# Decay attention and a softplus FFN on one core: TensorE's queue in emission order from the third block on

## The chip, the core and the metric

The kernel runs on one core of one Trainium2 chip. A core has five engines that work side by side, each through a queue of its own in strict program order: TensorE (PE, matrix products; its weight loads are shown as PEld), VectorE (DVE), ScalarE (ACT), GpSimd (POOL) and SyncE (SP, which here issues the DMAs). They meet at semaphores only. Matmuls write to PSUM, a small memory of eight banks, from which VectorE and ScalarE read. The metric is device microseconds of the whole program. "Faster" and "slower" mean against the kernel before.

## What is computed

For four sequences of 768 tokens and eight heads of 64, a linear attention with a decaying state is computed, and its output goes through a feed-forward network (FFN) with a softplus in the middle:

```python
for t in range(S):
    state = gamma[None, :, None, None] * state + np.einsum('bhd,bhe->bhde', k[:, :, t], v[:, :, t])
    y[:, :, t] = scale * np.einsum('bhd,bhde->bhe', q[:, :, t], state)
x = np.ascontiguousarray(attn_out.transpose(0, 2, 1, 3)).reshape(B * S, H * D)   # 3072 x 512
h = x @ w_in                                              # 512 -> 2048
g = np.maximum(h, 0.0) + np.log1p(np.exp(-np.abs(h)))     # softplus
return (g @ w_out).astype(np.float32)                     # 2048 -> 512
```

## The kernel before

**Units of attention.** The tokens are cut into 24 chunks of 128, and a unit is one chunk with four of its heads, 48 units in all. A unit passes through parts. `load_unit` and `decay` fetch q, k and v and scale them (L136, L153, L179, L180). `operands` turns k and q over on VectorE (L199) and splits them into high and low halves in one of two `kq` buffers (ScalarE L203, L206, L207; VectorE L204, L208). `scores` makes two score products `sc` on TensorE (L227), reduces each on VectorE (L228), masks the result on GpSimd (L229) and splits it into `ah` (ScalarE L233) and `al` (GpSimd L234). `new_state` adds to the running state in PSUM (L249). `outputs` makes the attention output `yp` on TensorE (L298 to L302; it reads `kq`, the state, `ah` and `al`), and ScalarE (L304, `xh`) and then VectorE (L306, `xl`) read it out of PSUM. `stack_state` copies the state out of PSUM (ScalarE L269, VectorE L271). The first 12 units go through simpler forms of these parts.

**Blocks of FFN.** The tokens are also cut into nine blocks: two of 256, six of 384 and one of 256. For a block of 384 there are 16 steps. A step's `hidden` is twelve matmuls into a buffer `hp` (L334 to L336); the softplus goes over VectorE (L341), ScalarE (L342), VectorE (L346), ScalarE (L348, `gh`) and GpSimd (L350, `gl`); and `second`, nine matmuls into three accumulators (L365 to L367), follows two steps later. At a block's end the accumulators are copied out (L379) and stored by DMA (L381).

**Interleaving.** The attention of a block runs beside the FFN of the block before it. `stages` (one call per step) emits `hidden`, about half of the step's ticks of attention, `second` of two steps before, and the other ticks. A unit takes four ticks: `operands`, `outputs` of the unit before, `scores`, `new_state`. Whole parts are emitted, one behind another.

**What sets the order in the queues.** The program is recorded in emission order, but a scheduler then lays out the instructions of each engine by a timeline of its own, in which an instruction that it expects to be ready may go ahead of one that it expects to wait. So an engine's queue differs from the emission order, and groups of matmuls are found inside one another. On the chip each queue is then fixed.

**PSUM.** `hp` has two banks, the accumulators three, the state one. `sc` and `yp` share the last two, the pool `ps_a`: each new tile takes one of the two, and its first matmul waits until the bank's last reader is done. Which of the two it takes is settled with the order.

```python
sc = ps_a.tile([P, 2, 2, C], F32, name="sc", tag="a")
yp = ps_a.tile([D, 2, NJ, C], F32, name="yp", tag="a")
```

Of the kernel before, what the change touches and what calls it, by code (L numbers as in the profile page):

```python
# [27 lines left out]
LAG = 2  # L28
# [5 lines left out]
def decay_attention_then_softplus_ffn(ctx: ExitStack, tc: tile.TileContext, q, k, v, w_in, w_out, qtab, vtab, gtab, out):  # L34
# [283 lines left out]
    def tick(n):  # L318
        for at, part in PARTS.items():
            u, r = divmod(n - at, PERIOD)  # L320
            if r == 0 and 0 <= u < len(units):
                part(u)
# [4 lines left out]
    def hidden(s):  # L327
        i, fs = steps[s]
        xh, xl = (x[:, :, spans[i][0]] for x in xring)
        hp = hps[s] = ps_h.tile([P, len(fs), BLOCKS[i]], F32, name="hp", tag="hp")  # L330
        for k, f in enumerate(fs):
            wt = win[f].rearrange("p t (c f) -> p t c f", c=ND)
            for d in range(ND):
                nc.tensor.matmul(hp[:, k], lhsT=wt[:, 0, d, :], rhs=xh[:, d, :], start=d == 0, stop=False)  # L334
                nc.tensor.matmul(hp[:, k], lhsT=wt[:, 0, d, :], rhs=xl[:, d, :], start=False, stop=False)  # L335
                nc.tensor.matmul(hp[:, k], lhsT=wt[:, 1, d, :], rhs=xh[:, d, :], start=False, stop=d == ND - 1)  # L336


    def softplus_1(s):
        sp = sps[s] = ffn.tile(list(hps[s].shape), F32, name="sp", tag="sp")  # L340
        nc.vector.tensor_scalar(sp.bitcast(U32), hps[s].bitcast(U32), 0x80000000, None, op0=ALU.bitwise_or)  # L341
        nc.scalar.activation(sp, sp, AF.Softplus)  # L342

    def softplus_2(s):
        g = sps[s]
        nc.vector.scalar_tensor_tensor(g, hps.pop(s), 0.0, g, op0=ALU.max, op1=ALU.add)  # L346
        gh = ffn.tile(list(g.shape), F32R, name="gh", tag="gh")
        nc.scalar.copy(gh, g)  # L348
        gl = ffn.tile(list(g.shape), F32R, name="gl", tag="gl")
        nc.gpsimd.tensor_tensor(gl, sps.pop(s), gh.bitcast(F32), op=ALU.subtract)  # L350
        gs[s] = gh, gl

    def second(s):
        i, fs = steps[s]
        NT = BLOCKS[i] // P
        gh, gl = gs.pop(s)
        begins = s == 0 or steps[s - 1][0] != i
        ends = s + 1 == len(steps) or steps[s + 1][0] != i
        if begins:
            acc[i] = [ps_o.tile([P, DM], F32, name=f"acc{t}", tag=f"acc{t}") for t in range(NT)]  # L360
        for k, f in enumerate(fs):
            wt = wout[f]
            for t in range(NT):
                ts = slice(t * P, (t + 1) * P)
                nc.tensor.matmul(acc[i][t], lhsT=gh[:, k, ts], rhs=wt[:, 0], start=begins and k == 0, stop=False)  # L365
                nc.tensor.matmul(acc[i][t], lhsT=gh[:, k, ts], rhs=wt[:, 1], start=False, stop=False)  # L366
                nc.tensor.matmul(acc[i][t], lhsT=gl[:, k, ts], rhs=wt[:, 0], start=False, stop=ends and f == fs[-1])  # L367
        if not ends:
            return
        for t in range(NT):  # L370
            if fs[-1] < NF - 1:
                part[i, t] = ffn.tile([P, DM], F32, name="part")
                (nc.scalar.copy if t % 2 else nc.vector.tensor_copy)(part[i, t], acc[i][t])
                continue
            o = ffn.tile([P, DM], F32, name="o", tag="o")
            if (i, t) in part:
                nc.vector.tensor_tensor(o, acc[i][t], part.pop((i, t)), op=ALU.add)
            else:
                (nc.scalar.copy if t % 2 else nc.vector.tensor_copy)(o, acc[i][t])  # L379
            row = int(FIRST[i]) + list(spans[i][1]).index(t) * P  # L380
            nc.sync.dma_start(out[row:row + P, :], o)  # L381
# [5 lines left out]
    steps = []  # L387
# [8 lines left out]
    done, loaded, converted = FIRST_TICK, 0, 0  # L396

    def convert_to(n):
        nonlocal loaded, converted
        while converted < min(NF, n):  # L400
            convert_weights(converted)
            converted += 1
            if loaded < NF:
                load_weights(loaded)
                loaded += 1
# [29 lines left out]
    def block_decays():  # L435
        own = (lo, slice(0, H, 2)), (up, slice(1, H, 2))
        for at in range(0, P, 32):
            for i in range(C // 32):
                nc.sync.dma_start(
                    qblocks[at:at + 32, 0, :, :, i].rearrange("p f m -> p (f m)"), qtab[i * 32:(i + 1) * 32, at // D:H:2]  # L440
                )
        for c in range(1, NC):
            for half, heads in own:
                old, new = (qblocks[half, t].rearrange("p f m i -> p (f m) i") for t in (c - 1, c))
                nc.gpsimd.tensor_tensor(new, old, gtab_sb[half, 0, heads].unsqueeze(2).broadcast_to(list(new.shape)), op=ALU.mult)
# [14 lines left out]
    plan = [0] * len(steps)  # L460
    for a, b in zip(starts, starts[1:]):
        i = steps[b][0]
# [8 lines left out]
    def stages(s, until):  # L471

        nonlocal done
        ok = lambda t: 0 <= t < len(steps)
        if ok(s):
            hidden(s)
            softplus_1(s)
            softplus_2(s)
        until = max(until, done)
        half = (done + until + 1) // 2  # L480
        while done < half:
            tick(done)
            done += 1
        if ok(s - LAG):
            second(s - LAG)
        while done < until:
            tick(done)
            done += 1

    for s, (i, fs) in enumerate(steps):  # L490
        if s == TURN:
            block_decays()
        convert_to(fs[-1] + 1)
        stages(s, plan[s])
        convert_to(2 * max(fs[-1] // 2 + 1, s + 1 if s < TURN else TURN + (s - TURN) // 2) + EARLY)
    for s in range(len(steps), len(steps) + LAG):
        stages(s, done)


# [28 lines left out]
```

## Time and profile before

| | |
|---|---|
| median of 3 runs | 683.71 us (682.54 to 686.89) |
| profiled execution | 683.14 us, of which the span is 681.3 us |
| TensorE busy | 661.6 us, 97% of the span |
| VectorE, ScalarE, GpSimd busy | 64%, 53%, 46% |
| granted TensorE clock | 0.997 on average |

A row of the timeline has start and length in us, engine, line, operation, what it writes and reads, how many were merged (xN), and in brackets the idle time ahead of it and what ended it. A matmul's length contains the time until its result has drained, so matmuls that follow one another overlap: the pace of TensorE is read from start to start. A row of the groups has, between the bars, the busy time in us and the mean in ns of one.

### The profile page before, as it was taken

The numbers are of one execution on the slowest core, as the hardware profiler recorded it, in microseconds if no ns is written. First come the engines' busy times: TensorE is split into PE (matmuls) and PEld (weight loads), VectorE is DVE, ScalarE is ACT, GpSimd is POOL, SyncE is SP. The second block draws the span as 40 slices with busy tenths as digits, with TensorE's granted clock in tenths as the row PEclk, the third lists the DMA queues.
The fourth block names the chain that finished last, engine by engine and source line by source line (L and its number), as shares of the span: only waits on it lengthen the run. The fifth ranks groups of instructions, "written<-read, shape, count | busy, mean of one in ns | idle before, by whom it ended". The sixth has DMA issues, their size and how long they took to land.

```text
span 681.3 us, 12857 instructions
## 1 busy us (share of the span) xinstructions
PE 661.6 (97%) x4146; PEld 600.3 (88%) x4146; DVE 436.1 (64%) x843; ACT 358.0 (53%) x808; POOL 316.5 (46%) x354
## 2 busy tenths in 40 slices
PE   7999899999999999999999999999999999999997
PEld 6898789988999999988999899988999899999996
DVE  5678698578567576785676766778666755432321
ACT  5788775545555355554555655455555545422221
POOL 5797666535435453454355344535344543332221
PEclk9999999999999999999999999999999999999999
DMA  9898653123112131222222222222212211000100
GB/s 246 237 270 231 184 141 72 26 69 82 35 36 53 29 95 26 40 39 64 48 38 54 37 77 42 37 36 53 76 37 38 36 33 47 1 1 1 46 1 32
DMA packets 153826, 46.75 MB, mean 69 GB/s; under 512 B 140448, under 2 KB 148640, under 8 KB 153760
## 3 DMA queue, kind: packets, MB, share of 16 engines
q1 hardware_dynamic: 153312, 45.93, 28.3%
q8 instruction: 33, 0.54, 0.3%
q14 instruction: 33, 0.27, 0.1%
q10 hardware_dynamic: 448, 0.01, 0.0%
HBM read 39.60 MB, written 6.29 MB: 67 GB/s over the span
## 4 chain that ended last, share of the span: by engine, by line
PE 52%; DVE 12%; SPq 11%; DMA 9%; issue 6%; ACT 5%; POOL 2%; DVEq 0%; ACTq 0%; POOLq 0%
SPq L136 10%; PE hp L334 8%; PE hp L336 8%; PE acc L365 8%; PE acc L367 8%; PE acc L366 8%; PE hp L335 8%; DVE kq L204 3%; DMA wout<-in_moe_w_out_dram 2%; DMA win<-in_moe_w_in_dram 2%; DMA kb<-in_k_dram 2%; DVE kq L208 2%; DMA qb<-in_q_dram 2%; DVE a L228 1%; DMA vn<-in_v_dram 1%
## 5 line engine op out<-in xcount | busy, mean ns | idle before, releaser
L350 POOL TENSOR_TENSOR gl<-sp,gh 128x384 fp32r<-128x384 f32 (+1 forms) x120 | 130.6, 1089 | 223.1 <-ACT gh L348 201.3
L334 PE MATMUL hp<-xh,winhl 128*128 128x384 f32 (+1 forms) x576 | 185.3, 322 | 2.4 <-DVE sp L346 1.9
L336 PE MATMUL hp<-xh,winhl 128*128 128x384 f32 (+1 forms) x576 | 184.7, 321 | 0.3 <-POOL winhl L99 0.3
L335 PE MATMUL hp<-xl,winhl 128*128 128x384 f32 (+1 forms) x576 | 183.7, 319 | 0.0
L365 PE MATMUL acc<-wouthl,gh 128*128 128x512 f32 x384 | 152.7, 398 | 0.0
L366 PE MATMUL acc<-wouthl,gh 128*128 128x512 f32 x384 | 151.8, 395 | 0.0
L367 PE MATMUL acc<-wouthl,gl 128*128 128x512 f32 x384 | 150.2, 395 | 0.0
L342 ACT ACTIVATE sp<-sp 128x384 f32<-128x384 f32 (+1 forms) x120 | 65.3, 546 | 137.7 <-DVE sp L341 134.6
L334 PEld LDWEIGHTS hp<-xh,winhl 128*128 128x128 f32 x576 | 108.8, 189 | 7.1 <-DVE sp L346 1.7
L335 PEld LDWEIGHTS hp<-xl,winhl 128*128 128x128 f32 x576 | 108.8, 189 | 3.7
L336 PEld LDWEIGHTS hp<-xh,winhl 128*128 128x128 f32 x576 | 108.7, 189 | 0.8 <-POOL winhl L99 0.5
L341 DVE TENSOR_SCALAR sp<-hp 128x384 uint32<-128x384 uint32 (+1 forms) x120 | 68.4, 573 | 61.1 <-PE hp L336 60.5
L348 ACT CAST gh<-sp 128x384 fp32r<-128x384 f32 (+1 forms) x120 | 64.1, 534 | 73.9 <-DVE sp L346 44.6
L346 DVE SCALAR_TENSOR_TENSOR sp<-hp,sp 128x384 f32<-128x384 f32 (+1 forms) x120 | 69.4, 580 | 34.6 <-ACT sp L342 33.6
L367 PEld LDWEIGHTS acc<-wouthl,gl 128*128 128x128 f32 x384 | 71.7, 188 | 14.4
L366 PEld LDWEIGHTS acc<-wouthl,gh 128*128 128x128 f32 x384 | 72.3, 188 | 11.1
L365 PEld LDWEIGHTS acc<-wouthl,gh 128*128 128x128 f32 x384 | 72.2, 188 | 10.9
L229 POOL TENSOR_SCALAR_AFFINE_SELECT a<-a 128x512 f32<-128x512 f32 x48 | 35.9, 749 | 48.5 <-DVE a L228 34.9
L228 DVE TENSOR_REDUCE a<-sc 128x256 f32<-128x512 f32 x72 | 48.9, 680 | 9.3 <-PE sc L227 7.8
L234 POOL TENSOR_TENSOR al<-a,ah 128x512 fp32r<-128x512 f32 x36 | 48.1, 1337 | 10.7 <-ACT ah L233 10.5
L204 DVE TENSOR_TENSOR kq<-kb,kq 64x256 fp32r<-64x256 f32 x72 | 49.7, 690 | 3.2 <-ACT kq L203 1.1
L199 DVE STREAM_TRANSPOSE kb<-kb 128x256 f32<-128x256 f32 x36 | 16.0, 445 | 51.8 <-DMA kb<-in_k_dram 39.8
(83 smaller groups left out, 994.0 us busy)
## 6 DMA issues: line engine op xcount, KB each, us to landing
win<-in_moe_w_in_dram SPq DMA_DIRECT2D x16, 512.0 KB, 4.5
wout<-in_moe_w_out_dram SPq DMA_DIRECT2D x16, 512.0 KB, 4.5
vn<-in_v_dram SPq DMA_DIRECT2D x48, 128.0 KB, 2.8
out_dram<-o SPq DMA_DIRECT2D x24, 256.0 KB, 2.1
kb<-in_k_dram SPq DMA_DIRECT2D x288, 16.0 KB, 1.7
qb<-in_q_dram SPq DMA_DIRECT2D x288, 16.0 KB, 1.7
vn<-in_k_dram SPq DMA_DIRECT2D x30, 128.0 KB, 2.4
qn<-in_q_dram SPq DMA_DIRECT2D x12, 128.0 KB, 4.7
```

Source lines behind the costliest of these rows:

```text
L136: nc.sync.dma_start(t[at:at + 32, h // 2], src[b, hf * HH + h, c * C:(c + 1) * C, d:d + 32].rearrange("(i t) d -> t i d", t=32))
L204: nc.vector.tensor_tensor(kq[oth, 0, par], kt[own], kq[own, 0, par].bitcast(F32), op=ALU.subtract)
L334: nc.tensor.matmul(hp[:, k], lhsT=wt[:, 0, d, :], rhs=xh[:, d, :], start=d == 0, stop=False)
L335: nc.tensor.matmul(hp[:, k], lhsT=wt[:, 0, d, :], rhs=xl[:, d, :], start=False, stop=False)
L336: nc.tensor.matmul(hp[:, k], lhsT=wt[:, 1, d, :], rhs=xh[:, d, :], start=False, stop=d == ND - 1)
L341: nc.vector.tensor_scalar(sp.bitcast(U32), hps[s].bitcast(U32), 0x80000000, None, op0=ALU.bitwise_or)
L342: nc.scalar.activation(sp, sp, AF.Softplus)
L346: nc.vector.scalar_tensor_tensor(g, hps.pop(s), 0.0, g, op0=ALU.max, op1=ALU.add)
L350: nc.gpsimd.tensor_tensor(gl, sps.pop(s), gh.bitcast(F32), op=ALU.subtract)
L365: nc.tensor.matmul(acc[i][t], lhsT=gh[:, k, ts], rhs=wt[:, 0], start=begins and k == 0, stop=False)
L366: nc.tensor.matmul(acc[i][t], lhsT=gh[:, k, ts], rhs=wt[:, 1], start=False, stop=False)
L367: nc.tensor.matmul(acc[i][t], lhsT=gl[:, k, ts], rhs=wt[:, 0], start=False, stop=ends and f == fs[-1])
```

## The change

The steps are split where the third block (index 2) begins. From there on the loop runs inside a manual schedule for TensorE: its instructions keep the order in which the kernel emits them. The other four engines are still ordered by the scheduler, against TensorE's new order. `convert_to` is not called in the second loop; all weights are converted by then. No instruction on tensors is added or removed, and the pools and buffers stay the same.

```diff
-    for s, (i, fs) in enumerate(steps):
+
+    ordered = next(s for s, (i, fs) in enumerate(steps) if i == 2)
+    for s, (i, fs) in enumerate(steps[:ordered]):
         if s == TURN:
             block_decays()
         convert_to(fs[-1] + 1)
         stages(s, plan[s])
         convert_to(2 * max(fs[-1] // 2 + 1, s + 1 if s < TURN else TURN + (s - TURN) // 2) + EARLY)
-    for s in range(len(steps), len(steps) + LAG):
-        stages(s, done)
+    with tc.manual_schedule(engines={mybir.EngineType.PE}):
+        for s in range(ordered, len(steps)):
+            stages(s, plan[s])
+        for s in range(len(steps), len(steps) + LAG):
+            stages(s, done)
```

How the queues move is shown at one unit, the eighteenth (`yp_2455` before, `yp_2457` now; a number behind a name tells one tile from another). TensorE before: the first matmul of `yp` stands inside a `second`, and the first score product of the next unit (`sc_2517`) inside the rest of it.

```order
L365 MATMUL acc2_2025<-wouthl_692,gh_2338 128x512
L300 MATMUL yp_2455<-ah_2374,vhl_2279 64x128
L366 MATMUL acc2_2025<-wouthl_692,gh_2338 128x512
L367 MATMUL acc2_2025<-wouthl_692,gl_2340 128x512
L227 MATMUL sc_2517<-kq0_84 128x256 x2
L334 MATMUL hp_2530<-xh_82,winhl_892 128x384
L335 MATMUL hp_2530<-xl_83,winhl_892 128x384
L336 MATMUL hp_2530<-xh_82,winhl_892 128x384
L301 MATMUL yp_2455<-al_2375,vhl_2279 64x128
```

The second product, `sc_2521`, stands behind the end of `yp_2455` and nine more matmuls of `hidden`; it waits for VectorE's reduction of `sc_2517`. TensorE now, from the last matmul of `yp` on:

```order
L302 MATMUL yp_2457<-ah_2376,vhl_2281 64x128
L365 MATMUL acc0_2025<-wouthl_692,gh_2340 128x512
L366 MATMUL acc0_2025<-wouthl_692,gh_2340 128x512
L367 MATMUL acc0_2025<-wouthl_692,gl_2342 128x512
L365 MATMUL acc1_2026<-wouthl_692,gh_2340 128x512
L366 MATMUL acc1_2026<-wouthl_692,gh_2340 128x512
L367 MATMUL acc1_2026<-wouthl_692,gl_2342 128x512
L365 MATMUL acc2_2027<-wouthl_692,gh_2340 128x512
L366 MATMUL acc2_2027<-wouthl_692,gh_2340 128x512
L367 MATMUL acc2_2027<-wouthl_692,gl_2342 128x512
L227 MATMUL sc_2519<-kq0_84 128x256 x2
L227 MATMUL sc_2523<-kq0_84 128x256 x2
```

The parts stand whole: `yp`, the nine matmuls of one `second`, and both products side by side. `sc_2519` takes the free bank of `ps_a` and `sc_2523` the one of `yp_2457`. The waits show in the same place of the unit before it, where a `hidden` stands in front of the products, again on TensorE now:

```order
L335 MATMUL hp_2323<-xl_83,winhl_683 128x384
L336 MATMUL hp_2323<-xh_82,winhl_683 128x384
L227 MATMUL sc_2367<-kq1_85 128x256 [waits PE_49]
L227 MATMUL sc_2367<-kq1_85 128x256
L227 MATMUL sc_2371<-kq1_85 128x256 [waits DVE_49,PE_49]
L227 MATMUL sc_2371<-kq1_85 128x256
L365 MATMUL acc0_2025<-wouthl_554,gh_2197 128x512 [waits Activation_49]
```

The second product's wait on VectorE is for the read-out of that unit's `yp` (L306). ScalarE's queue up to the read-out of the eighteenth unit's `yp`, before:

```order
L342 ACTIVATE sp_2447<-sp_2447 128x384
L348 CAST gh_2451<-sp_2447 128x384
L206 CAST kq1_85<-qb_2351 64x256
L207 CAST kq1_85<-qb_2351 64x256
L206 CAST kq1_85<-qb_2351 64x256
L269 CAST st1_2480<-stp_93 64x128 x2
L207 CAST kq1_85<-qb_2351 64x256
L304 CAST xh_82<-yp_2455 64x2x128 x2
```

And now:

```order
L348 CAST gh_2408<-sp_2404 128x384
L206 CAST kq1_85<-qb_2353 64x256
L342 ACTIVATE sp_2449<-sp_2449 128x384
L207 CAST kq1_85<-qb_2353 64x256
L206 CAST kq1_85<-qb_2353 64x256
L269 CAST st1_2482<-stp_93 64x128 x2
L207 CAST kq1_85<-qb_2353 64x256
L304 CAST xh_82<-yp_2457 64x2x128 x2
```

The four copies into `kq1`, which wait until `yp` has read the values there, and the state copies stand ahead of L304 in both; the softplus L342 of the step at hand has moved in among them.

## The prediction

> **What bounds the kernel now.** I read the page first, then busy time by stretches of the span, then TensorE's waits, then the timeline around one attention unit.
>
> ```profile
> span 681.3 us, 12857 instructions
> PE 661.6 (97%) x4146; PEld 600.3 (88%) x4146; DVE 436.1 (64%) x843; ACT 358.0 (53%) x808; POOL 316.5 (46%) x354
> ```
>
> ```profile
> core 0: us, PE busy (x) PEld busy (x) DVE busy (x) ACT busy (x) POOL busy (x), PEclk, DMA share, GB/s
> 0.00:200.00 200.00, 188.53 (x1253) 171.45 (x1254) 144.04 (x274) 128.44 (x271) 122.54 (x146) 0.99 0.54 138
> 200.00:560.00 360.00, 355.50 (x2188) 322.33 (x2186) 249.17 (x492) 192.06 (x462) 161.57 (x179) 1.00 0.23 47
> 560.00:640.00 80.00, 80.00 (x486) 73.22 (x485) 33.31 (x64) 29.39 (x63) 24.07 (x24) 1.00 0.05 17
> 640.00:682.00 42.00, 37.54 (x227) 33.31 (x225) 9.60 (x14) 8.11 (x13) 8.37 (x7) 0.99 0.05 20
> ```
>
> TensorE is the bound: 97% of the span. Of the 19.7 us in which it is idle (681.3 - 661.6), about 11.5 lie before 200 us (200 - 188.53), which the change hardly touches, and about 4.5 behind 640 us, where only the last block's FFN is left. Between 200 and 560 us, where attention and FFN are interleaved and the new order applies, only 4.5 us are idle (360 - 355.50). So the change can win little there: the matmuls are the same ones.
>
> ```profile
> engine line waited for: us in total, times, longest us
> PE sc L227 <- DVE a L228: 3.8, 5, 1.5
> PE yp L300 <- ACT ah L233: 0.4, 1, 0.4
> PE hp L334 <- DVE sp L346: 0.3, 1, 0.3
> ```
>
> These are TensorE's waits from 195 to 600 us, and they add to the same 4.5 us. Nearly all is one kind: a score product (`sc`, L227) that waits until VectorE has reduced (L228) the one before it, because both use the same PSUM buffer. One of them close up:
>
> ```profile
> 375.33 0.44 PE L366 MATMUL acc<-wouthl,gh 128*128 128x512 f32 x1
> 377.31 0.50 PE L227 MATMUL sc<-kq 128*128 128x256 f32 x2 [1.54 <-DVE a L228]
> 377.65 0.39 PE L367 MATMUL acc<-wouthl,gl 128*128 128x512 f32 x1
> ```
>
> The L367 behind the product had its operands, yet it ran only behind it. A waiting matmul holds everything that stands behind it, so what counts is what stands between a producer and its consumer.
>
> **What goes.** The 4.5 us are waits of the old order; the new one has none of these interleavings. Idle time shows only where a gap outlasts the end of the matmul before it (the gap above is 1.98 us from start to start, 1.54 shown), so I take 5 us as gone, with ends of 0 and 9 (twice what is shown).
>
> **What comes.** In the old order the first product of a unit is pulled ahead of the rest of the preceding `yp` (the attention output) and the second stands a block of FFN later; both use one of the two buffers of `ps_a`, and `yp` has the other to itself. In the new order the two products stand side by side, each needs a buffer, and the second takes the one of the `yp` just before. So its wait on VectorE is for L306, the last reader of that `yp`. How late is that? The same unit as in the quoted order, in the trace of before (a row's first two columns are start and busy time, here with rows of all engines):
>
> ```profile
> 197.78 0.22 PE L300 MATMUL yp<-ah,vhl 128*64 128x128 f32 x1
> 198.37 0.40 PE L227 MATMUL sc<-kq 128*128 128x256 f32 x2
> ...
> 199.81 0.41 ACT L206 CAST kq<-qb 64x256 fp32r<-64x256 f32 x1 [0.97 <-PE yp L298]
> 200.09 0.22 PE L302 MATMUL yp<-ah,vhl 128*64 128x128 f32 x1
> 200.15 0.40 PE L334 MATMUL hp<-xh,winhl 128*128 128x384 f32 x1
> 200.24 0.41 ACT L207 CAST kq<-qb 64x256 fp32r<-64x256 f32 x1
> 200.67 0.40 ACT L206 CAST kq<-qb 64x256 fp32r<-64x256 f32 x1
> 201.10 0.53 ACT L269 CAST st<-stp 64x128 fp32r<-64x128 f32 x2
> 201.65 0.40 ACT L207 CAST kq<-qb 64x256 fp32r<-64x256 f32 x1
> 201.81 0.40 PE L227 MATMUL sc<-kq 128*128 128x256 f32 x2
> 202.04 0.40 PE L365 MATMUL acc<-wouthl,gh 128*128 128x512 f32 x1
> 202.08 0.74 ACT L304 CAST xh<-yp 64x256 fp32r<-64x256 f32 x2
> 202.87 0.85 DVE L306 TENSOR_TENSOR xl<-yp,xh 64x256 fp32r<-64x256 f32 x2
> ```
>
> The last matmul of `yp` starts at 200.09 and its buffer is free at 203.72 (202.87 + 0.85): 3.63 us later. ScalarE sets this. Its four copies of the next `kq` (L206, L207) cannot begin before `yp` has read the old one, and they and the two state copies (L269) stand ahead of `xh` (L304) in its queue. They do so in the new order too.
>
> How much TensorE has to do meanwhile is read from a block of FFN:
>
> ```profile
> 308.44 0.39 PE L365 MATMUL acc<-wouthl,gh 128*128 128x512 f32 x1
> ...
> 310.53 0.33 PE L334 MATMUL hp<-xh,winhl 128*128 128x384 f32 x1
> ...
> 312.63 0.39 PE L365 MATMUL acc<-wouthl,gh 128*128 128x512 f32 x1
> ```
>
> Nine output matmuls take 2.09 us, twelve hidden ones 2.10. One product takes 0.23 (201.81 to 202.04) and a `yp` matmul 0.06 (200.09 to 200.15). With one block between, TensorE reaches the second product 0.06 + 2.09 + 0.23 = 2.38 us after the last `yp` matmul starts, and stands until 3.63: 1.25 us, and 1.30 with 0.05 from a release to the next start (L304 ends at 202.82, L306 starts at 202.87).
>
> From the third block on the new order goes in rounds of three units: behind `yp` stand nine output matmuls; or nine output and twelve hidden ones; or twelve hidden ones. Where two blocks stand, the cover is 4.47 us and I charge nothing. From the attention of the fourth block to that of the eighth there are twenty units with one block, ten of each kind. Their queues differ:
>
> ```profile
> L342 ACT ACTIVATE sp<-sp 128x384 f32<-128x384 f32 x96 | 50.2, 524 | 107.7 <-DVE sp L341 104.9 <-POOL vn L180 2.7
> L269 ACT CAST st<-stp 64x128 fp32r<-64x128 f32 x60 | 15.6, 260 | 1.6 <-PE stp L249 0.7
> ```
>
> - Eight with output matmuls behind `yp` have a softplus (L342) between the copies as well, 0.55 with its gap: 1.30 + 0.55 = 1.85 each, 14.8 us.
> - Two of that kind, in a sequence's last chunk, have the softplus and no state copies (0.55 less): 1.30 each, 2.6.
> - Six with hidden matmuls have the queue of the rows above: 1.30 each, 7.8.
> - Two of that kind have no state copies there: 0.75 each, 1.5.
> - Two, in a sequence's first chunk, have no `kq` copies gated by `yp` ahead of L304: nothing.
>
> That is 26.7 us. What else holds VectorE ahead of L306 comes on top:
>
> ```profile
> DVE kb L199 <- DMA kb<-in_k_dram: 39.8, 23, 4.4
> DVE o L379 <- DMA out_dram<-o: 8.7, 5, 2.1
> ```
>
> At the start of four blocks the first of these units has the last copy of the block's result (L379) ahead of the softplus on VectorE, and that copy waits for an output DMA, 1.7 us at a time (8.7/5). I take 1 us each of it, 4 us, between 0 and 1.7. A transposition (L199) of freshly loaded `k` stands ahead too and waits 1.7 us in 23 of 36 units; the loads are issued earlier against TensorE's progress when TensorE stands still, so I take none of it, and half of it for twenty units (17 us) as the upper end.
>
> ```profile
> L234 POOL TENSOR_TENSOR al<-a,ah 128x512 fp32r<-128x512 f32 x36 | 48.1, 1337 | 10.7 <-ACT ah L233 10.5
> ```
>
> The other edges cost nothing. `hidden` needs a buffer that is free after L341, L342 and L346, three steps of about L342's 0.52 us, with three blocks (6.3 us) between; `yp` needs `al`, four steps behind its products of which L234 with 1.34 us is the longest, and again three blocks stand between; the output matmuls need `gl` of two steps earlier. SP, POOL and the DMAs keep their work, only re-timed.
>
> **Sum.** 683.1 us (the profiled execution: span 681.3 and 1.8 around it) - 5 + 26.7 + 4 = 708.8; against the median of 683.7, half a microsecond more, I say 708. That is 3.6% slower.
>
> One rule bears on it. The row first: the evacuation takes 3.63 us and the block behind it 2.09. The Trainium skill (Perfetto Trace Analysis, Matmuls) says that independent groups of matmuls should rotate through different PSUM banks, so that the evacuation of one overlaps the next group's matmuls. By that rule alone the new rotation is right and the sum would be 683 - 5 = 678; I go by the rows, where the overlap is too short.
>
> **Rivals.**
>
> *The buffer is free in time, and the new order wins.* Were L304 to go first on ScalarE, L304 and L306 would need 0.74 + 0.85 = 1.59 us, and with 0.2 for the matmul's own end the buffer is free before 2.38 us. Then nothing is lost and 5 to 9 us are won: 678 to 674. It decides where the release falls under 2.38 us. For it: before rarely shows TensorE waiting for `yp` to be read. Against: ScalarE's order, which is fixed, and the gate on L206. 0.10, half of it beyond 1%.
>
> *Late loads.* L199 waits its 1.7 us ahead of L306 or of the softplus in all twenty: 709 + 34 = 743. For it: 39.8 us of such waits now. Against: a slower TensorE gives SP more time. 0.10.
>
> *The clock drops.*
>
> ```profile
> 0.00:40.00 40.00, 34.03 (x218) 30.64 (x219) 26.02 (x60) 27.98 (x58) 27.40 (x47) 0.96 0.90 235
> ```
>
> In the first 40 us, with 6 us idle, the granted clock is 0.96, that is 1.6 us lost; from 200 to 560 us, with gaps up to 1.5 us, it is 1.00. Did each of the twenty waits cost what the start does, 32 us would be added: 741. Against it are the waits' sizes, 1.85 at most. 0.03. The Trainium skill (TensorE: Matmul & The Clock Gate, "Why this matters for your kernels") asks for no idle gaps over about 3 us; by that rule too these waits are short enough, and the traced clock agrees for 1.5 us.
>
> *The products are late instead.* If VectorE's reduction is late, `al` reaches `yp` late, 1 us in 34 units: 742. The trace shows 0.4 us on ScalarE's `ah` now. 0.03.
>
> *It does nothing.* What moves is cancelled by the re-timed queues of the other engines: 683. 0.04.
>
> **How the numbers follow.** My forecast has 0.70. The low end: only the eight longest and two of 1.30 (17.4), less 9, is 691.5. The high end: 709 and half of the L199 waits, 726. Range 691 to 726. About 1% is what a measurement of this kernel can tell from no change, 676.9 to 690.5. Faster: half of the first rival, 0.05. Within 1%: the other half, the 0.04 and 0.03 from below the range's low end: 0.12. Slower: 0.83.
>
> **What would show it.** In TensorE's waits L227 <- DVE `xl` L306, about 18 times, 1 to 2 us each, 20 to 35 us in total, and the waits on L228 gone; PE idle between 200 and 590 us near 30 us; behind nine output and twelve hidden matmuls no wait; the granted clock at 1.00. I am wrong if L227 does not wait for L306, if the waits are under 0.5 us, or if `hp` or `yp` turn out to wait for more.

## The result, and the profile after

The changed kernel takes 716.09 us (median of 4 runs, 713.56 to 718.3) against 684.95 (682.54 to 686.89) for the kernel before: a ratio of 1.045, 95% interval 1.0403 to 1.0497. The forecast was 708 in a range of 691 to 726. The profiled execution of the changed kernel took 717.04 us, 715.3 of them its span: 34.0 us more span than before.

The page's rows for the span and the engines, of the kernel after:

```profile
span 715.3 us, 12828 instructions
PE 667.5 (93%) x4146; PEld 607.1 (85%) x4146; DVE 427.9 (60%) x843; ACT 360.7 (50%) x808; POOL 317.2 (44%) x354
```

The matmuls are the same 4146. TensorE's idle time has gone from 19.7 to 47.8 us (715.3 - 667.5), which is 28.1 of the 34.0; its busy time has gone from 661.6 to 667.5, which is the other 5.9. Equal matmuls that take longer point to the clock. By stretches of the span:

```profile
core 0: us, PE busy (x) PEld busy (x) DVE busy (x) ACT busy (x) POOL busy (x), PEclk, DMA share, GB/s
0.00:200.00 200.00, 182.77 (x1201) 165.93 (x1202) 141.16 (x269) 125.84 (x266) 118.12 (x142) 0.98 0.53 137
200.00:560.00 360.00, 334.69 (x2041) 304.96 (x2040) 224.88 (x457) 180.98 (x428) 150.91 (x166) 0.99 0.22 44
```

From 200 to 560 us TensorE is idle for 25.3 us where it was idle for 4.5, and before 200 us for 17.2 where it was 11.5. What it waits for, over the whole span after (line waited at, engine and line waited for, us in total, times, longest):

```profile
engine line waited for: us in total, times, longest us
PE sc L227 <- DVE xl L306: 29.3, 18, 3.2
PE hp L335 <- DVE xl L306: 3.4, 1, 3.4
...
PE sc L227 <- DVE a L228: 0.5, 1, 0.5
```

The first row is the wait that the prediction named. One of the eighteen close up, in the timeline after (start, busy time, engine, line): a unit that has nine output matmuls behind its `yp`, and the softplus in ScalarE's queue.

```profile
254.89 0.41 ACT L206 CAST kq<-qb 64x256 fp32r<-64x256 f32 x1 [2.38 <-PE yp L298]
255.17 0.22 PE L302 MATMUL yp<-ah,vhl 128*64 128x128 f32 x1
255.20 0.52 ACT L342 ACTIVATE sp<-sp 128x384 f32<-128x384 f32 x1
255.23 0.45 PE L365 MATMUL acc<-wouthl,gh 128*128 128x512 f32 x1
...
256.60 0.53 ACT L269 CAST st<-stp 64x128 fp32r<-64x128 f32 x2
257.16 0.41 ACT L207 CAST kq<-qb 64x256 fp32r<-64x256 f32 x1
257.36 0.40 PE L227 MATMUL sc<-kq 128*128 128x256 f32 x2
257.59 0.74 ACT L304 CAST xh<-yp 64x256 fp32r<-64x256 f32 x2
258.36 0.85 DVE L306 TENSOR_TENSOR xl<-yp,xh 64x256 fp32r<-64x256 f32 x2 [0.60 <-ACT xh L304]
259.36 0.47 PE L227 MATMUL sc<-kq 128*128 128x256 f32 x2 [1.60 <-DVE xl L306]
```

The second row is the last `yp` matmul, at 255.17. TensorE has done the block and the first product by 257.6 and stands until L306 has read the buffer, at 259.21 (258.36 + 0.85), that is 4.04 us behind the `yp` matmul. ScalarE's L304 waited for nothing but its own queue: from 254.89 on ScalarE is busy without a break with copies of the next `kq`, the softplus and the state.

Three of the eighteen are longer, 2.7 to 3.2 us. Rows of all engines around one of them, after:

```profile
403.65 0.74 ACT L304 CAST xh<-yp 64x256 fp32r<-64x256 f32 x2
...
404.56 0.45 DVE L199 STREAM_TRANSPOSE kb<-kb 128x256 f32<-128x256 f32 x1 [4.16 <-DMA kb<-in_k_dram]
406.40 0.85 DVE L306 TENSOR_TENSOR xl<-yp,xh 64x256 fp32r<-64x256 f32 x2
407.39 0.47 PE L227 MATMUL sc<-kq 128*128 128x256 f32 x2 [3.14 <-DVE xl L306]
```

Here `xh` is ready at 404.39, but VectorE has stood for 4.16 us at a transposition (L199) of `k` that is loaded for a later unit, and L306 stands behind it and behind two more of VectorE's instructions (L208 and L271, 0.83 and 0.59 us), which came late for the same reason. The second row of the waits has the same cause. It lies at the seam, where the strict order begins and `hidden` of the third block reads the last unit's `xl`:

```profile
150.90 0.45 DVE L199 STREAM_TRANSPOSE kb<-kb 128x256 f32<-128x256 f32 x1 [2.86 <-DMA qb<-in_q_dram]
151.84 0.83 DVE L306 TENSOR_TENSOR xl<-yp,xh 64x256 fp32r<-64x256 f32 x2
152.73 0.44 PE L335 MATMUL hp<-xl,winhl 128*128 128x384 f32 x1 [3.44 <-DVE xl L306]
```

In the clock, short stretches at half speed show. Windows set on them, after (the granted clock is the third figure from the end):

```profile
153.10:156.50 3.40, 3.40 (x11) 2.92 (x10) 2.75 (x5) 0.77 (x2) 2.47 (x3) 0.50 0.41 88
211.20:214.60 3.40, 3.40 (x13) 3.40 (x12) 2.27 (x4) 1.09 (x3) 1.71 (x3) 0.50 0.17 27
407.50:410.90 3.40, 3.40 (x19) 3.04 (x20) 3.27 (x7) 1.66 (x4) 0.81 (x1) 1.00 0.19 30
538.80:545.60 6.80, 6.14 (x18) 5.30 (x19) 4.53 (x10) 2.36 (x5) 3.14 (x4) 0.50 0.13 21
```

Each stretch at 0.50 stands at one of the longest waits: the 3.4 us that ended at 152.7, the 2.7 at 210.5 and the 3.2 at 539.5. The 3.1 us that ended at 407.4 was followed by full speed (third row). The trace of before has no such stretch between its first 20 us and its end. Together they are 13.6 us at half clock, so at most 6.8 us lost (TensorE still stood in the first 0.7 us of the last one); 5.9 us was the growth of TensorE's busy time.

So of the 34.0 us: +29.3 the waits for the read-out of `yp`, +3.4 the one at the seam, -3.7 the old waits (L228 and L300 had 4.2 us, 0.5 are left), and about +6 the clock. That makes 35, one more than measured.

### The profile page after: what moved, and what is told of

It reads as the page before. It is cut to its first block, busy times and chain, and to the rows that moved or that the text cites. A ratio compares the mean times of both kernels' runs of the same rounds, so it can differ in the third digit from the quotient of the medians.

```text
span 715.3 us, 12828 instructions
## 1 busy us (share of the span) xinstructions
PE 667.5 (93%) x4146; PEld 607.1 (85%) x4146; DVE 427.9 (60%) x843; ACT 360.7 (50%) x808; POOL 317.2 (44%) x354
## 4 chain that ended last, share of the span: by engine, by line
PE 60%; DVE 11%; SPq 9%; DMA 7%; ACT 6%; issue 4%; POOL 1%; DVEq 0%; ACTq 0%; POOLq 0%
PE acc L365 9%; PE acc L366 9%; PE acc L367 9%; PE hp L336 9%; PE hp L334 9%; PE hp L335 9%; SPq L136 8%; DMA kb<-in_k_dram 3%; DVE xl L306 3%; DMA wout<-in_moe_w_out_dram 2%; DVE kq L204 2%; ACT xh L304 2%; PE sc L227 2%; DVE a L228 2%; PE stp L249 1%
## 5 line engine op out<-in xcount | busy, mean ns | idle before, releaser
L342 ACT ACTIVATE sp<-sp 128x384 f32<-128x384 f32 (+1 forms) x120 | 65.4, 545 | 121.7 <-DVE sp L341 121.0
L341 DVE TENSOR_SCALAR sp<-hp 128x384 uint32<-128x384 uint32 (+1 forms) x120 | 69.1, 577 | 93.0 <-PE hp L336 91.7
L348 ACT CAST gh<-sp 128x384 fp32r<-128x384 f32 (+1 forms) x120 | 64.0, 534 | 58.3 <-PE acc L366 32.8
L366 PEld LDWEIGHTS acc<-wouthl,gh 128*128 128x128 f32 x384 | 73.0, 190 | 11.7
L365 PEld LDWEIGHTS acc<-wouthl,gh 128*128 128x128 f32 x384 | 73.0, 190 | 11.6
L227 PE MATMUL sc<-kq 128*128 128x256 f32 x144 | 28.3, 295 | 29.8 <-DVE xl L306 29.3
L206 ACT CAST kq<-qb 64x256 fp32r<-64x256 f32 x72 | 29.1, 404 | 50.9 <-PE yp L298 41.8
L227 PEld LDWEIGHTS sc<-kq 128*128 128x128 f32 x144 | 23.1, 190 | 33.9 <-issue 30.3
```

Of the source, the lines that this page charges most:

```text
L227: nc.tensor.matmul(sc[:, par], lhsT=kq[:, 0, par, j, :], rhs=kq[:, 1:, par, j, :], start=True, stop=True)
```

## The experiments

Three theories were set against each other.

- **A, the bank.** The second product stands because it takes the PSUM bank of the `yp` just before, and ScalarE reads that `yp` out late, since other copies stand ahead in its queue.
- **B, the strict order itself.** An order that can't slip costs time wherever any producer is late; with the L306 waits gone, others would take their place and the time would stay.
- **C, the seam.** The time goes where the strict order begins, not in the rounds behind it.

**Read-out first on ScalarE.** The order of TensorE stays as in the kernel after; an ordering edge without a semaphore puts ScalarE's copies of the next `kq` and of the state behind the read-out of `yp`.

```
+    def behind(n, made):
+        if n in read:
+            tc.add_manual_dep(made.ins, read[n].name, ..., reason="xh first")
-            nc.scalar.copy(kq[own, 1, par], qt[own])
-            nc.scalar.copy(kq[oth, 1, par], qt[own])
+            behind(n - 2, nc.scalar.copy(kq[own, 1, par], qt[own]))
+            behind(n - 2, nc.scalar.copy(kq[oth, 1, par], qt[own]))
-            nc.scalar.copy(st[own, par], s)
+            behind(n, nc.scalar.copy(st[own, par], s))
-            nc.scalar.copy(xh[own], yp[:, par])
+            read[n] = nc.scalar.copy(xh[own], yp[:, par]).ins
```

> The changed kernel, with one edit: on ScalarE the read-out of `yp` (L304) is put ahead of the next `kq` copies (L206, L207) and of the state copies (L269) by an order-only dependency; no work is added. Theory A (TensorE waits for `yp`'s bank because L304 stands behind five or six copies on ScalarE): the read-out is through 1.7 to 2.4 us after `yp`, inside the 2.38 us that one block covers, so the 18 waits of L227 on L306 (29.3 us) shrink to under 5 us, the clock drops that follow long waits go with them (some 4 us), and the time is 680 to 690 us. Theory B (the two products side by side are the fault whatever ScalarE does, and the wait would pass to VectorE's queue): the waits stay over 20 us and the time over 705.

Measured: 690.59 us beside 685.4 for the kernel before, ratio 1.0093 (1.0056 to 1.0129). About 25 of the 31 us come back with TensorE's order untouched. The wait and one unit in its timeline (the read-out is L309 here, its remainder L311, the last `yp` matmul L307):

```profile
PE sc L227 <- DVE xl L311: 8.9, 8, 1.8
```

```profile
411.33 0.22 PE L307 MATMUL yp<-ah,vhl 128*64 128x128 f32 x1
411.59 0.74 ACT L309 CAST xh<-yp 64x256 fp32r<-64x256 f32 x2
412.36 0.85 DVE L311 TENSOR_TENSOR xl<-yp,xh 64x256 fp32r<-64x256 f32 x2
412.91 0.41 ACT L206 CAST kq<-qb 64x256 fp32r<-64x256 f32 x1
413.51 0.64 PE L227 MATMUL sc<-kq 128*128 128x256 f32 x4
```

The read-out starts 0.26 us behind the last `yp` matmul instead of 2.42, the bank is free 1.88 us behind it instead of 4.04, and both products run back to back (x4 in one row). The waits fall from 29.3 to 8.9 us, and some 6 of the 25 us are the clock, whose mean is 0.997 here and 0.988 after. B, by which the time would have stayed, does not hold. In the waits that are left L311 stands behind the transposition L199 on VectorE, as in the long ones above.

**One product per step.** The other cure on TensorE's side: the second product and what hangs on it are emitted one step later than the first, with a block between the two.

```
-            for j in range(NJ):
-                ...
+            product(kq, a, 0)
+            pending[n] = a
     ...
-    PARTS = {-6: load_unit, -2: decay, 0: operands, 2: scores, 3: new_state, 5: stack_and_outputs}
+    PARTS = {-6: load_unit, -2: decay, 0: operands, 2: scores, 3: second_product_and_state, 5: stack_and_outputs}
```

> The changed kernel, with the second score product and what follows from it (mask, `ah`, `al`) emitted one tick later than the first, so that a block of FFN stands between the two; ScalarE's order is left as it is. Theory A: the second product meets `yp`'s bank 4.3 us or more after `yp` and finds it read, so the waits of L227 on L306 go (under 3 us). But `yp` follows its last product by two blocks (4.2 us) instead of three, and from that product to the end of `al` the trace of after has 4.4 to 6.5 us, so a new wait of L301 on `al` of 0.3 to 1.5 us comes in some 20 units: 690 to 705 us. Theory B: no difference to after, 712 to 718.

Measured: 701.56 us, ratio 1.0254 (1.0215 to 1.0293), inside the expectation, though 4.4 us of the L306 waits are left, more than expected.

```profile
PE yp L317 <- POOL al L250: 10.4, 14, 1.4
PE sc L234 <- DVE xl L322: 4.4, 6, 1.6
```

The time between the products frees the bank, but `al` is now made a step later and reaches `yp` late in 14 units. Since this edit moves two things, it shows only that the second product's distance from `yp` sets the L306 wait, and that the chain from the products to `al` had no whole step to spare.

**A bank of its own for `yp`.** `ps_a` has two buffers that products and `yp` take in turn. Here `yp` keeps one and the products the other.

```
-    ps_a = ctx.enter_context(tc.tile_pool(name="ps_a", bufs=2, space=bass.MemoryType.PSUM))
+    ps_a = ctx.enter_context(tc.tile_pool(name="ps_a", bufs=1, space=bass.MemoryType.PSUM))
     ...   (the tiles of the first 12 units take the two in turn)
-        yp = ps_a.tile([D, 2, NJ, C], F32, name="yp", tag="a")
+        yp = ps_a.tile([D, 2, NJ, C], F32, name="yp", tag="y")
```

> The changed kernel, with `ps_a` cut in two pools of one bank: `yp` has one to itself, both products share the other (the first 12 units take turns). Theory A (the bank is what TensorE waits for): the waits of L227 on L306 vanish altogether, and in their place the second product waits for the reduction of the first in every unit, 34 times 0.8 us or more, 27 to 50 us in all, so the time stays within 705 to 730. Theory B' (the second product waits for something else that ends with L306, not for the bank): the waits on L306 stay as they are.

Measured: 756.8 us, ratio 1.1079 (1.1024 to 1.1135), above what was expected. The row of the L306 wait is gone, as A says; but the second product now waits for the first to be reduced, and far longer:

```profile
PE sc L227 <- DVE a L228: 62.1, 33, 3.1
```

```profile
258.63 0.40 PE L227 MATMUL sc<-kq 128*128 128x256 f32 x2
258.87 0.74 ACT L309 CAST xh<-yp 64x256 fp32r<-64x256 f32 x2
259.64 0.85 DVE L311 TENSOR_TENSOR xl<-yp,xh 64x256 fp32r<-64x256 f32 x2 [0.60 <-ACT xh L309]
260.52 0.69 DVE L228 TENSOR_REDUCE a<-sc 128x256 f32<-128x512 f32 x1
261.27 0.50 PE L227 MATMUL sc<-kq 128*128 128x256 f32 x2 [2.24 <-DVE a L228]
```

The first product ends near 259, and its reduction takes 0.69 us; yet VectorE does it only behind the remainder of `yp` (L311 here), which stands ahead in its queue and waits for ScalarE. The late read-out holds TensorE by way of VectorE's queue even where no bank is shared. The expectation had priced the reduction alone.

**The order from the sixth block on.** Half the dose.

```
-    ordered = next(s for s, (i, fs) in enumerate(steps) if i == 2)
+    ordered = next(s for s, (i, fs) in enumerate(steps) if i == 5)
```

> The changed kernel, but TensorE keeps the emission order only from the sixth block (index 5) on. Theory A: the cost lies in the attention of each block that is ordered, four one-block units each; of 20 such units 8 remain, so 7 or 8 waits on L306, 11 to 14 us, and with about 2 us for the clock the time is 694 to 701. Theory C (it is the seam between the two orders that costs): as after, 712 to 718, or with the seam where it is cheaper, as before.

Measured: 697.92 us, ratio 1.0195 (1.0136 to 1.0254):

```profile
PE sc L227 <- DVE xl L306: 12.0, 7, 3.3
```

The whole dose has 29.3 us in 18 waits. The loss grows with the number of units under the order, 1.7 us of wait for each of the 7 and 1.6 for each of the 18, so it isn't the seam's (C).

**The read-out made longer.** Each of the two copies of L304 is issued twice, 0.74 us more work on ScalarE between `yp` and the release of its bank.

```
             nc.scalar.copy(xh[own], yp[:, par])
+            nc.scalar.copy(xh[own], yp[:, par])
```

> The changed kernel, with each read-out copy of `yp` on ScalarE (L304) made twice, 0.74 us more of work in front of L306 per unit. Theory A: every one-block unit's wait on L306 grows by about 0.74 us, and the two-block units (cover 4.47 us, release 3.8) begin to wait by a few tenths; 18 to 28 waits, 40 to 55 us in all, the longer of them over 2.5 us, so the half-clock stretches (four in after, one of them at the start) become six or more; 728 to 745 us. If the waits were not on this read-out, the work would lie beside TensorE's and the time would stay at 712 to 720.

Measured: 751.82 us beside 684.55, ratio 1.0972 (1.0928 to 1.1016); above the expectation. TensorE's waits:

```profile
PE sc L227 <- DVE a L228: 37.6, 19, 3.8
PE sc L227 <- DVE xl L307: 12.4, 12, 1.9
```

50.0 us of waits at the second product instead of 29.8, but not as 0.74 us more in each unit. Two other copies of ScalarE (L211 and L349) have come to stand among the four, so the bank of `yp` is free 5.55 us behind its last matmul where it was 4.04. Ten of the twelve waits on the remainder (L307 here) stand in rounds with two blocks of matmuls, which had no such wait: their cover is 4.47 us, and TensorE now idles 1.0 us in each. In rounds with one block most waits are put down to L228: there the second product takes the bank of the first (in one it starts at 173.57, before L307 does at 173.82), so the buffers go in another turn than after. The run is no clean dose; what it shows is that the two-block rounds begin to wait once the release falls behind their cover. The rest is the clock: its mean is 0.970, which is 22.5 us of a span of 750.9 against 8.6 us after (0.988 of 715.3). The longest wait here is 3.8 us.

**The ScalarE order in the old kernel.** The edges of the first experiment put into the kernel before, to see whether they help by themselves.

```
     # in the kernel before, TensorE's order as it was
     ...   (as in the first experiment)
+            behind(n - 2, nc.scalar.copy(kq[own, 1, par], qt[own]))
     ...
+            behind(n, nc.scalar.copy(st[own, par], s))
```

> The kernel before (TensorE free to be reordered), with the same order on ScalarE as in the first experiment: L304 ahead of the `kq` and state copies. Theory A: there the second product does not take `yp`'s bank, so nothing waits for L304 and there is nothing to win: the waits of TensorE stay 4 to 6 us and the time 680 to 690 us. If ScalarE's order were a cost of its own in any order of TensorE, this would be faster than before by several us.

Measured: 689.06 us, ratio 1.0064 (1.0043 to 1.0086): no gain, a little slower. The read-out's place in ScalarE's queue wins time only with the new order of TensorE. The waits for the FFN (`hp` L339 on VectorE's `sp`) are 4.6 us in 5, where before had 1.9 in 3. The profiled execution, 685.36 us, is the fastest of the twelve, so its trace does not show where the rest goes; it was not followed.

**Read-out first on VectorE too.** To the first experiment's edges comes one on VectorE: the transposition of `k` (L199) for a unit may not stand ahead of the remainder of `yp` of four units earlier.

```
-            nc.vector.transpose(blocks, blocks)
+            made = nc.vector.transpose(blocks, blocks)
+            if x is rest[0] and n - 4 in last:
+                tc.add_manual_dep(made.ins, last[n - 4].name, ..., reason="xl first")
-            nc.vector.tensor_tensor(xl[own], yp[:, par], xh[own].bitcast(F32), op=ALU.subtract)
+            last[n] = nc.vector.tensor_tensor(xl[own], yp[:, par], xh[own].bitcast(F32), op=ALU.subtract).ins
```

> The first experiment's kernel (emission order on TensorE, `yp` read out first on ScalarE), with one more order-only dependency on VectorE: the transposition of the `k` of the unit four later (L199), which waits for a load, goes behind `xl` (L306). In the first experiment 8.9 us of waits on L306 were left, all in units where `xh` was through in 0.8 to 1.0 us and L306 began only 1.5 to 3.2 us after `yp`. Theory A with the loads as what is left: the waits fall to 0 to 4 us and the time to 681 to 688, level with before; if something else holds VectorE, they stay at 7 to 10 us and the time at 689 to 692.

Measured: 681.22 us, ratio 0.9948 (0.9928 to 0.9967). The waits from 195 to 600 us and the stretch from 200 to 560:

```profile
PE yp L309 <- POOL al L237: 2.8, 6, 0.7
PE sc L230 <- DVE xl L314: 0.3, 1, 0.3
```

```profile
200.00:560.00 360.00, 356.89 (x2208) 326.57 (x2207) 241.86 (x496) 197.39 (x465) 162.82 (x181) 1.00 0.23 47
```

With the bank free in time TensorE is idle for 3.1 us in 360, less than the 4.5 before. The kernel is then half a per cent faster than before. Against the old kernel with the same ScalarE edges (689.06) it wins 1.1%. Neither figure is the strict order's alone: VectorE's edge was not tried in the kernel before, so what it would win there is not known.

**The seam a step later.** The same with the strict order beginning one step later, so that the `hidden` of the seam wait comes ahead of it.

```
-    ordered = next(s for s, (i, fs) in enumerate(steps) if i == 2)
+    ordered = next(s for s, (i, fs) in enumerate(steps) if i == 2) + 1
```

> As the kernel with both read-outs first, but the emission order begins one step later, so that the first `hidden` of the third block is not yet held in order behind the last `yp` of its own block. Expected: the wait of the first hidden matmuls (L335) on L306 at the seam (3.4 us in after, 1.4 in the first experiment) goes, all else equal: 1 to 2 us less than the kernel beside it, 679 to 687; if the seam only moves, no difference.

Measured: 679.9 us, ratio 0.9935 (0.9912 to 0.9958). The seam's wait is gone from the trace, but the difference from the run before (679.9 and 681.2) is within their intervals: what the seam costs by itself (C) is too small to be told here. This is the fastest version that was run.

**VectorE's edge alone, and the kernel after again.** The last two runs part the late loads from ScalarE's queue: the kernel after with the VectorE edge only, and the kernel after itself, unchanged, on the same chip.

```
     # ScalarE's order as in the kernel after
+                tc.add_manual_dep(made.ins, last[n - 4].name, ..., reason="xl first")
```

> The changed kernel with the order-only dependency on VectorE alone: the transposition of `k` (L199) of the unit four later goes behind L306; ScalarE's order is that of the changed kernel. In after three of the 18 waits on L306 are far over the rest (2.7, 3.1 and 3.2 us against 1.0 to 1.7), and ahead of L306 a transposition waits for its load there. If the loads make them, they fall to the size of their kind (1.3 and 1.7), the 29.3 us to 24 to 26, and the two half-clock stretches that came with two of them (10.2 us long, 5.1 lost) go: 704 to 709 us. If not, 712 to 718 with three long waits.

> The changed kernel itself, on the same chip as the run beside it. As measured, 712 to 718 us, with waits of 27 to 32 us on L306. If the half-clock stretches stand where a wait of over 2.5 us ends, they stand behind such waits again, though not necessarily behind the same ones.

Measured: 703.9 us, ratio 1.0274 (1.0224 to 1.0324), and 715.45, ratio 1.0433 (1.0388 to 1.0477). The wait in the one and in the other:

```profile
PE sc L230 <- DVE xl L309: 24.7, 19, 1.6
```

```profile
PE sc L227 <- DVE xl L306: 29.0, 18, 3.1
```

The edge takes away 4.3 us of these waits and cuts the longest from 3.1 to 1.6 us; the seam's falls from 3.2 to 0.9. That is 6.6 us, where 11.5 are won. The rest is the clock: its mean goes from 0.990 (7.1 us of the span of 714.6) to 0.997 (2.1 of 702.1). So the late loads cost some 11 us in the kernel after, and ScalarE's queue the 23 between 703.9 and 681.2. With ScalarE's edges put in first they are 25 us for ScalarE (716.09 to 690.59) and 9 for VectorE (690.59 to 681.22).

## Why the prediction was right

**The wait and its cause: right.** It was to be L227 on L306, about 18 times, 20 to 35 us; it is 18 times and 29.3 us. The read-out put first on ScalarE brought most of it back, and the separate bank made its row vanish.

**The terms by kind of unit: right in their sum, uneven by kind.** From the second product's delay in the timeline, the units with the softplus and the state copies in the queue lose 1.76 us each where 1.85 was taken, and those with hidden matmuls and state copies 1.33 where it was 1.30, late loads apart; the rounds with two blocks show no wait, as charged. The two small kinds were off. The two units with the softplus and no state copies lose 1.1 us each where 1.30 was taken. The two with hidden matmuls and no state copies lose 1.5 and 1.2 us where 0.75 was: the copy `gh` (L348) stands ahead of the others on ScalarE, and in one of them a late load stands on VectorE as well. Measured like the terms, from start to start, the eighteen delays add to 32.1 us (29.3 is the part that shows as idle time). The three long waits hold some 5 us more than their units were given; the other 27.1 stand against the sum's 26.7.

**The 4 us for the output copy (L379): wrong, it is nothing.** The copy does wait for its DMA. In the unit shown above, at a block's start, the timeline after has it on VectorE:

```profile
253.73 0.69 DVE L379 COPY o<-acc 128x512 f32<-128x512 f32 x1 [1.83 <-DMA out_dram<-o]
254.34 0.55 DVE L341 TENSOR_SCALAR sp<-hp 128x384 uint32<-128x384 uint32 x1
```

But the softplus behind it on ScalarE stands behind the first `kq` copy, which waits for `yp` until 254.89, and VectorE had its step ahead of the softplus (L341) done by then. The two delays lie side by side, and the sum added them. The four units at a block's start lose 1.77 us, like the others of their kind.

**The late loads (L199): taken as nothing, and wrong.** The reasoning was that a slower TensorE gives the loads more time. In most units that holds. In three it doesn't, and at the seam it doesn't: 5 us of longer waits, 2.3 us at the seam (what the VectorE edge took from it), and the clock behind them. The run with the VectorE edge puts the whole at 11.5 us, within the 17 that the prediction kept as the upper end.

**The seam: not in the prediction.** It looked at the rounds behind the start of the order and not at the first `hidden` in it, which stands behind the last unit's L306 and waits for 3.4 us.

**The clock: wrong.** It was to stay at 1.00, with the argument that 1.85 us was the longest wait. The premise fell: the late loads made waits of up to 3.4 us, and half clock came at three of the four longest. Nor would the argument have been safe with it: half clock stands behind a wait of 0.95 us (ended at 148.4) in the run with VectorE's edge alone, and behind one of 1.7 us (ended at 377.0) in the run with the order from the sixth block. The loss here is some 6 us, where this rival had been priced at 32 with a chance of 0.03, for a drop at all twenty waits.

**What goes: right in size.** 3.7 us of the old waits went where 5 were taken. The last versions show the gain with the loss taken away: 3.3 and 4.7 us under the kernel before beside them (681.2 and 679.9 against 684.55), where the rival with a buffer free in time had 5 to 9.

The 716 lie 8 us above the forecast. Late loads and seam are about 8 and the clock some 6, less the 4 of L379. That makes 10; where the other 2 went was not followed. The mechanism was the one named, but it is luck that the 4 us for L379, which the kernel does not pay, made up for part of what was left out. The forecast took late loads and clock as two rivals, each at its best value in the sum. They hang together in part: in the profiled executions beside each other, the kernel after has four half-clock stretches and the one with VectorE's edge has one, at the seam.

**The rule on banks** (the Trainium skill, Perfetto Trace Analysis, Matmuls: independent groups rotate through different PSUM banks) would have given 678. The kernel after does rotate, over two buffers, and loses 29.3 us. The runs show what has to come with it here: the read-out must fit into the matmuls between. At 4.04 us behind `yp` it doesn't, at 1.88 it does, with the same banks.

## What to carry to other kernels

Before an order on the bounding engine is fixed, look up for each PSUM bank who reads it last and what stands ahead of that reader in its own queue: the time from the last matmul to the release, not the reader's own duration, must be shorter than the matmuls up to the next use of the bank. Where it is too long, the cure that won most here is an order edge on the reading engine: 25 of 31 us, where the other order of the matmuls that was tried won back 14. Any instruction on such a reading engine that waits for a DMA belongs behind the read-out, since under a strict order TensorE stands until it is through: 4.16 us at one transposition became a wait of 3.14 us at the product.

## What the runs showed of the hardware

Half clock came in stretches of 3.4 us or twice that, each costing half its length; in the two profiled executions of the kernel after, behind waits of 2.4 to 3.4 us once the first 20 us are over. In the second execution four places show it. Windows set on two of them, and on 16.6 to 20.0 us:

```profile
16.60:20.00 3.40, 2.10 (x17) 1.62 (x17) 1.92 (x4) 2.61 (x6) 3.12 (x4) 1.00 1.09 324
209.80:213.20 3.40, 3.40 (x12) 3.40 (x13) 2.91 (x5) 1.42 (x3) 1.77 (x2) 0.51 0.19 29
407.80:411.20 3.40, 3.40 (x12) 2.75 (x11) 2.58 (x5) 1.74 (x4) 1.43 (x3) 0.50 0.15 23
```

The one at 209.8 stands behind a wait of 2.7 us, the one at 407.8 behind one of 3.1; of the other two, the 3.2 us at the seam and one of 2.4 us that ended at 539.7. The same wait of 3.1 us near 407 brought no drop in the first execution (third row of the clock windows above), with the same kernel. From 16.6 to 20.0 us it is the other way round: 0.50 in the first execution, 1.00 in the second (first row). So the length of a gap alone doesn't decide it. Nor is it a safe limit from below: the run with one product per step has drops at 356 and 442 us where no wait is longer than 1.6 us (waits of 0.6 and 1.1 us stand just ahead of each), and in the run with VectorE's edge alone half clock stands behind the seam's wait of 0.95 us (ended at 148.4), while the kernel before, with waits of up to 1.5 us behind its first 20 us, has none there.

The Trainium skill (TensorE: Matmul & The Clock Gate, "What's actually happening") tells of two states, half and full, and of an activity window of 3413 ns that runs free of the kernel's start. The two levels and the length of the stretches agree with it, and a free-running window could explain that one wait of 3.1 us has a drop in one execution and none in the other; no run here shows where the windows lie. Its table has the clock fall after an idle window of about 3.4 us; here it fell at waits of 2.4 and 2.7 us.
